# An adaLN block with dilated local attention and a SiLU FFN: rows of 448 held as four overlapping tiles of 128

## The chip, the cores and the metric

The kernel runs on one core of a Trainium2 chip. A core has TensorE (PE in the profile; its weight loads are the row PEld), VectorE (DVE), ScalarE (ACT), GpSimd (POOL) and SyncE (SP, which here only issues DMAs). They run side by side, each in its own fixed order, and wait for each other through semaphores. The metric is the device time of one execution in microseconds (us), lower is better. Times of one instruction are given in us or ns as the profile has them.

## The reference

One transformer layer, sequence 2048, width 448, 16 heads of 28, FFN width 1792, all inputs bf16:

```python
mod = silu(c) @ w_mod                      # 448 -> 6 * 448: sa, ca, ga, sb, cb, gb
h = layernorm(x) * (1 + ca) + sa
x = x + ga * attention(h)                  # qkv = h @ wqkv; out = o @ wo
h = layernorm(x) * (1 + cb) + sb
x = x + gb * (silu(h @ w1) @ w2)
```

Attention is local and dilated: position s sees s, s-2, ..., s-14 (8 keys, those below 0 masked), with logits scaled by 28^-0.5 and a softmax over the 8.

## The kernel before

**Tiling.** The sequence is split by parity into two streams of 1024, so that the dilated window becomes 8 neighbours. It is worked in four chunks (`NC`) of 2 x 256 positions, and attention in nine blocks (`BLOCKS`) of 128 keys and 112 queries (128 for block 0), for each parity. A width of 448 is contracted on TensorE as three tiles of 128 rows and a rest of 64. `tile 3` of a transposed activation holds rows 384 to 447 in 64 partitions. Matmuls on 64 partitions come in pairs, one on the lower half of the array and one on the upper half, so the rest has to be present in both halves: each modulation (L491 to L497, L513 to L519) writes it twice, once to partitions 0 to 63 and once to 64 to 127. The weights' rests (`wqkv3`, `w13`) are loaded to the two halves by two DMAs each. `xn` is 512 wide with 64 zero columns.

**Stages of a chunk.** Statistics of x (`stat`, L428, on DVE), reciprocal square root on POOL (`rstd`, L442 to L449), the normalized rows `xn` (`norm`, L456 on ACT or L458 on DVE), a transpose (chunk 0: on TensorE, L486; others: DMA transposes issued by SP, L510), the modulation (`mod`). Then the q and k projections (`project`, L596, two groups of 16 matmuls, each over two large PSUM buffers), whose results ACT or DVE evict (L600), and v (L620, evicted at L609). For each block and parity: logits (L648), exp on ACT (L656), mask on DVE (L680), attention times v (L706), normalization on DVE (L712), DMA transpose of o (L716). Output projection (L740), and addition to x with the row sums (L743). The FFN of a chunk: sums and squares for the second norm (L438 on ACT), transposes by DMA, modulation (L519 on DVE, L517 on ACT), first matrix with SiLU on ACT (L766, L768, L772), second matrix (L790), addition (L795), store.

**PSUM.** Three large buffers (`big`, two banks each) serve the transposes of chunk 0, q/k and v projections, logits, output projection and the FFN's first matrix. Two small ones (`one`) serve attention times v, the modulation's matmuls and the FFN's second matrix.

**The start.** 11 matmuls on zeros (`WARM`, L369) and then 3 (`JUNK`) behind each of chunk 0's four transposes keep TensorE active until data is there. The modulation vectors need `w_mod` (two DMAs for the first part); `pad` (L525 to L530) spreads the q/k weights of 28 columns a head to 32.

**Order.** The work is written as steps (`P.op`) with a cost and dependencies. A planner can order them, but for the kernel that runs, the order is given by the string `ORDER`: the numbers of the steps, with `v` (DVE) or `a` (ACT) where a step may go to either. Each engine gets its instructions in that order. `SEQ` sets the order in which attention blocks (e) and FFN chunks (s) are created, with one switch of ACT's table (exp or SiLU) at each change. In the string before, attention of blocks 0 to 3 comes ahead of FFN chunk 0, blocks 4 and 5 among its second matrix, 6 to 8 among that of FFN chunk 1.

Of the kernel before, what the change touches and what calls it, by code (L numbers as in the profile page):

```python
# [10 lines left out]
ALU = mybir.AluOpType  # L11
# [4 lines left out]
D = 448  # L16
H = 16
DH = 28
F = 1792
# [16 lines left out]
WARM, JUNK = 11, 3  # L36
HOW1 = ("bbbb", "bbbb", "bbbb", "bbbb")
HOW2 = ("ssss", "ssss", "ssss", "ssss")
SEQ = "e0 e1 e2 e3 s0 e4 e5 s1 e6 e7 e8 s2 s3"
# [3 lines left out]
    "0 4 5 91 79 3 2 1 80 81 92 93 94v 65 66 67 68 69 8 6 7 95a 82 83 9 96 97 98 99v 10 11 101 102 12 15 13 21 19 17 14 18 22 85 89v 86 87v 100a 16 20 90a "  # L43
    "88a 103 104 106v 105a 114 74 73 70 78 71 116a 29 30 158a 141 115 142 143 144a 145a 31 27 25 23 107 32 146 147 33 37 24 28 117 26 176 148 72 175 149v "
    "181 177 39 180 178v 151 40 34 209 215 118a 150a 152 108 109 119 153 110a 112a 179v 84 156v 155v 154v 157v 192v 210 35 59 49 111 182 75 76 50 113 120 "
    "121a 63 47 45 183v 214 184v 38 186 185 55 41 43 42 36 46 48 211 245 122 246 123a 124 125v 247 212a 248 165 166 169v 130 167a 213a 132 77 216 168 170 "
    "264 265 266 252 253 254 249 267 250 191v 255 171 268 172a 217a 188a 269 159 219 131 61 251 62 161a 190v 189v 162 44 160 163v 164 271 256 272 273 126 "
    "279 280 281 64 257 274 218v 127v 282 205 259 286 275 206a 287 288 276 277 187 270 173 283 57 220 278 58 289 284 285 174a 133 260 261 262 263 56 258 "
    "298 290 299 300 291 301 223v 128 305 306 207 307 317 319 208a 137 225v 293 302 303 129 308 222a 318 226a 199 201a 320 294 224a 309 51 304 53 136 296 "
    "295 310 311 323 221 324 325 52 202 312 54 292 60 297 200 203a 139 321v 322v 204 329 193 194 195a 197a 198 326 134 328v 327v 138 330 313 314 315 316 "  # L50
    "196 331 334a 332v 239 241 333v 335v 354 427 242a 429 140 240v 342 343 355 344 346 345 356 336 337 338 428 430 431v 135 339 347 340 348 349 350 341 "
    "351 389 357 358 352 359 365 353 390 391 396 397 392 360 366 398 408 409 410 361 367 399 393 415 394 416 368 417 400 395 369 401 227 228 418 229a 231a "
    "232 230 411 419 420 432a 403 422 439 404 406 405 433 434 435 436 402 381 412 243 413 414 438v 407 233 234 373 437v 440 442v 445v 443v 235a 244a 423 "
    "382 237a 424 425 362 363 364 238 236 370 426 371 444a 464 465 466 458 460 461 372 459 556 462 446 447 448 450 558 449 463 452 453 454 455 451 499 383 "
    "384 385 374 375 376 456 386 457 500 501 377 506 467 468 507 502 503 504 518 508 557 559 469 470 519 525 509 378 505 379 380 471 510 511 483 484 485 "
    "486 560a 520 526 521 522 527 561a 512 528 487 523 537 513 421 387 388 514 538 539 515 516 529 491 544 492 562 564 563 565 530 493 494 488 568 524 545 "
    "546 441 489 517 531 540 495 532 566v 567v 475 541 569 476 533 542 547 548 477 478 574a 573v 571v 572v 575 576 534 535 628 630 629 631 490 536 549 577 "
    "496 543 551 632v 633v 640 578 593 552 579 479 700 594 553 554 634 635 636 637 639v 638v 641 595 580 620 581 604 582 583 645v 643v 480 472 646v 644v "
    "584 555 587 588 585 589 591 586 592 590 621 605 622 606 607 647 648 623 473 497 498 474 649 650 653 654 624 596 597 657 658 608 651 655 625 609 610 "
    "570 656 652 642 626 627 481 611 665 676 598 599 600 601 602 482 603 659 660 661 666 663 677 692 693 694 695 678 679 696 680 681 697 698 668 669 612 "  # L60
    "613 614 615 670 699 682 616 671 672 673 617 684 685 686 687 618 683 688 667 674 619 675 664 662 550 689 690 701 702 703 691 "
# [12 lines left out]
def half(j):  # L74
    return slice(K3 * j, K3 * j + K3)


def rows_of(k, j=0):

    return half(j) if k == 3 else slice(0, 128)  # L80
# [118 lines left out]
def layer(ctx, tc, io, safe):  # L199
# [3 lines left out]

# [33 lines left out]
    wv = ct([128, 3, D], "wv")  # L237
    wqkv3 = ct([128, 2, D], "wqkv3")
# [43 lines left out]
    for i in range(2):  # L282
        V.memset(ob[0][i][:, D:512], 0.0)
        V.memset(ob[1][i][:, 0:K3], 0.0)
        V.memset(xn[i][:, :, D:512], 0.0)
# [21 lines left out]

    begin = P.op(("sp", 1630.0), none)

    def load(kb, out, in_, after=()):  # L310
        a = P.op(("sp", max(400.0, kb / 0.31)), lambda o: nc.sync.dma_start(out=out, in_=in_), [begin] + list(after))
        return P.op(("none", 500.0), none, [a])
# [13 lines left out]
    ld_ma = load_mod(0, 2 * D + K3)  # L326
    late = [P.op(("sp", 800.0), none, ld_ma[:1])]
    rest = A_wqkv[384:D, :].rearrange("k (a n) -> k a n", a=3)
    ld_qk = [[load(224, wqk[:, kk, :], A_wqkv[128 * kk:128 * kk + 128, 0:2 * D], late)] for kk in range(3)]
    ld_qk.append([load(56, wqkv3[half(j), 0, :], rest[:, j, :], late) for j in range(2)])  # L330
    ld_v = [load(336, wv[:], rows3(A_wqkv[:, 2 * D:3 * D]), late)] + [load(56, wqkv3[half(j), 1, :], rest[:, 2, :], late) for j in range(2)]
    ld_x += [[load(448, x_all[:, 4 * k:4 * k + 4, :].rearrange("p (i t) d -> p i (t d)", t=2), x_view[k], late)] * 2 for k in range(1, NC)]
    ld_mo, ld_mb, ld_m2 = load_mod(2 * D + K3, 3 * D, late), load_mod(3 * D, 5 * D + K3, late), load_mod(5 * D + K3, 6 * D, late)
    ld_m2 = ld_mb + ld_m2
    ld_o = [load(336, wo[:, 0, 0:3, :], rows3(A_wo), late), load(56, wo[half(0), 0, 3, :], A_wo[384:D, :], late)]
    ld_1 = [load(448, w1[:, kk, :], B_w1[128 * kk:128 * kk + 128, :], late) for kk in range(3)]
    ld_1 += [load(112, w13[half(h), :], B_w1[384:D, h * F // 2:(h + 1) * F // 2], late) for h in range(2)]
# [31 lines left out]
    w_last = P.op(("pe", 213.0 * WARM), lambda o: warm_up(WARM), [w_first], mac=213.0 * WARM)  # L369

# [7 lines left out]
    cc = P.op(("pe", 60.0), c_cols, [sc_op, w_last], take=("one",))  # L378
# [3 lines left out]
    def mod_cols(vecs, dst0, loads):  # L382
# [3 lines left out]
        def mm(o):  # L386
            ps[0] = one.tile([128, 2, KT], F32, name="ps_m", tag="one")
            for i, v in enumerate(vecs):
                for j in range(KT):
                    c0 = v * D + 128 * j  # L390
                    for k in range(KT):
                        T.matmul(ps[0][:, i, j:j + 1], lhsT=wmod[:, k, c0:c0 + 128], rhs=scT[:, k:k + 1], start=(k == 0), stop=(k == KT - 1))
# [23 lines left out]
    class Norm:  # L416


        def __init__(self, us, src, after=(), n=2, how="bbbb", scratch=None):
# [31 lines left out]
            def norm(o, j, b):  # L451
                if j == 0:
                    self.box["x"] = xn[o["slot"]["xn"]]
                out_, in_ = self.box["x"][:, j, 0:D], x_all[:, us[j], :]
# [5 lines left out]
            for j in range(0, 4, n):  # L460
# [8 lines left out]
                for i in at:  # L469
                    self.nr.append(P.op(either(640.0, 310.0), lambda o, j=i, b=b: norm(o, j, b), [r] + self.nr[:1], take=() if i else ("xn",)))  # L470

        def on_pe(self, order, out_of, view, waits, junk_n=0, two=False):
# [6 lines left out]
            def tr(o, j):  # L479
# [7 lines left out]
                if junk_n:  # L487
                    warm_up(junk_n)
# [81 lines left out]
    def norm1(k):  # L570
# [5 lines left out]
        def out_of(rows, kt):  # L576
            return h[rows, :, kt, 128:128 + CP]
# [346 lines left out]
```

## Time and profile before

| | us |
|---|---|
| median of 14 runs (185.12 to 187.61) | 186.94 |
| the profiled execution | 187.28 |
| its span, first to last instruction | 185.4 |
| mean granted TensorE clock | 0.983 |

The span is what the trace covers; 1.9 us of the profiled execution lie around it. Groups of the page that the change bears on, each with the line, engine, operation, result and operand, shapes and count, then busy us in total and mean ns of one, then the idle time before them and what ended it:

```profile
L456 ACT ACTIVATE xn<-x_all,nm,rs 128x448 bf16<-128x448 bf16 x11 | 8.3, 760 | 8.5 <-POOL nm L449 6.8 <-POOL nm L447 1.8
L458 DVE TENSOR_SCALAR xn<-x_all,mv,rs 128x448 bf16<-128x448 bf16 x21 | 7.6, 388 | 18.0 <-POOL rs L445 17.9
L519 DVE TENSOR_SCALAR h<-h,modc 128x512 bf16<-128x512 bf16 x14 | 5.2, 408 | 8.5 <-DMA h<-xn 8.5
L519 DVE TENSOR_SCALAR h<-h,modc 64x512 bf16<-64x512 bf16 x10 | 4.1, 405 | 0.3
L517 ACT ACTIVATE h<-h,modc 128x512 bf16<-128x512 bf16 x4 | 3.3, 832 | 2.8 <-DMA h<-xn 2.8
L367 PE MATMUL ps_w<-both 128*128 128x512 bf16 x22 | 7.5, 486 | 1.3 <-DVE both L272 1.2
```

The norms read 448 elements a row, the modulations write 512 columns, on 128 partitions or, for the rest, on 64. `ps_w` are the matmuls on zeros.

### The profile page before, as it was taken

How to read it: one execution, taken by the hardware profiler on the slowest of the kernel's cores; microseconds unless marked ns; L12 is line 12 of the kernel's file. 1: busy time of each engine (PE TensorE's matmuls, PEld its weight loads, DVE VectorE, ACT ScalarE, POOL GpSimd, SP SyncE). 2: the span in 40 equal slices, each digit the busy share in tenths (PEclk: the TensorE clock that was granted, in tenths of full speed). 3: DMA queues.
4: the chain of work that ended last, by engine and by line, in shares of the span. 5: the costliest groups of instructions: out<-in, count | busy, mean ns of one | idle time of the engine just before them, and what ended most of it. 6: DMA issues, size and time to landing. Idle time of an engine off the chain costs nothing.

```text
span 185.4 us, 3540 instructions
## 1 busy us (share of the span) xinstructions
PE 169.7 (92%) x1401; PEld 76.8 (41%) x1402; DVE 97.2 (52%) x223; ACT 115.5 (62%) x151; POOL 28.5 (15%) x86
## 2 busy tenths in 40 slices
PE   7769896999999999999999999989989999999950
PEld 2333333345643333454443345455334444445520
DVE  7579888968997802097433015788752222012120
ACT  3176979788899597896385689666496611650000
POOL 1736536000043002000200000402022000000000
PEclk9999999699999999999999999999999999999997
DMA  5995698979465200002440001223421501000120
GB/s 177 327 339 183 149 279 173 240 224 172 104 147 160 57 0 4 0 0 53 106 108 4 0 0 50 55 55 79 106 57 24 108 2 50 0 25 4 50 74 16
DMA packets 33119, 17.42 MB, mean 94 GB/s; under 512 B 24328, under 2 KB 32584, under 8 KB 33096
## 3 DMA queue, kind: packets, MB, share of 16 engines
q1 hardware_dynamic: 33088, 17.13, 36.6%
q8 instruction: 13, 0.21, 0.5%
q14 instruction: 10, 0.08, 0.2%
q10 hardware_dynamic: 8, 0.00, 0.0%
HBM read 9.12 MB, written 1.84 MB: 59 GB/s over the span
## 4 chain that ended last, share of the span: by engine, by line
PE 53%; ACT 18%; DVE 9%; POOL 6%; DMA 5%; issue 4%; SPq 1%; ACTq 0%; DVEq 0%; POOLq 0%
PE ps_h L766 18%; PE ps_y L790 12%; PE ps_qk L596 8%; ACT p L656 6%; PE ps_v L620 5%; PE ps_wo L740 4%; PE ps_h L768 4%; DMA h<-xn 3%; ACT screp L438 3%; POOL rs L445 2%; ACT xn L456 2%; PE ps_o L706 2%; DMA w<-in_B_w_dram 2%; ACT both L772 2%; DVE x_all L743 2%
## 5 line engine op out<-in xcount | busy, mean ns | idle before, releaser
L790 PE MATMUL ps_y<-w,both 128*128 128x448 bf16 x224 | 46.1, 353 | 0.2 <-DVE o L712 0.2
L772 ACT ACTIVATE both<-ps_h 128x1024 bf16<-128x1024 f32 x28 | 27.9, 1023 | 20.2 <-PE ps_h L768 12.2
L766 PE MATMUL ps_h<-h,w 128*128 128x512 bf16 x168 | 40.2, 380 | 0.2 <-DVE h L519 0.2
L656 ACT ACTIVATE p<-ps_l 128x896 bf16<-128x896 f32 (+1 forms) x36 | 30.8, 936 | 2.2 <-PE ps_l L648 2.1
L795 DVE TENSOR_TENSOR ot<-ps_y,x_all 128x448 bf16<-128x448 f32 x16 | 9.9, 622 | 38.2 <-PE ps_y L790 38.2
L790 PEld LDWEIGHTS <-both 128*128 128x128 bf16 x224 | 20.8, 98 | 19.9 <-issue 0.9
L766 PEld LDWEIGHTS <-w 128*128 128x128 bf16 x168 | 15.3, 98 | 22.1 <-issue 6.1
L680 DVE TENSOR_TENSOR p<-p,maskb 128x1792 bf16<-128x1792 bf16 (+1 forms) x18 | 19.7, 1101 | 8.1 <-ACT p L656 8.0
L596 PE MATMUL ps_qk<-h,wp 128*128 128x512 bf16 (+1 forms) x96 | 21.2, 390 | 1.2 <-ACT h L495 1.2
L600 ACT CAST qk<-ps_qk 128x1024 bf16<-128x1024 f32 x14 | 13.9, 1011 | 5.3 <-PE ps_qk L596 5.2
L458 DVE TENSOR_SCALAR xn<-x_all,mv,rs 128x448 bf16<-128x448 bf16 x21 | 7.6, 388 | 18.0 <-POOL rs L445 17.9
L596 PEld LDWEIGHTS <-wp 128*128 128x128 bf16 (+1 forms) x128 | 9.5, 98 | 17.2 <-issue 8.9
L438 ACT ACTIVATE screp<-x_all,mv 128x448 bf16<-128x448 bf16 x16 | 10.7, 671 | 6.1 <-POOL mv L435 5.8
L519 DVE TENSOR_SCALAR h<-h,modc 128x512 bf16<-128x512 bf16 (+1 forms) x24 | 9.1, 407 | 8.8 <-DMA h<-xn 8.5
L456 ACT ACTIVATE xn<-x_all,nm,rs 128x448 bf16<-128x448 bf16 x11 | 8.3, 760 | 8.5 <-POOL nm L449 6.8
L740 PE MATMUL ps_wo<-wo,oT 128*128 128x448 bf16 (+1 forms) x64 | 13.0, 354 | 0.5 <-ACT both L772 0.5
L712 DVE TENSOR_TENSOR o<-ps_o,rc 112x448 bf16<-112x448 f32 (+1 forms) x18 | 11.2, 624 | 0.6
L445 POOL TENSOR_TENSOR rs<-rs,negh 128x2 f32<-128x2 f32 x16 | 11.3, 709 | 1.3
L706 PEld LDWEIGHTS <-p 128*128 128x128 bf16 x288 | 9.1, 96 | 4.9 <-DVE p L680 1.8
L706 PE MATMUL ps_o<-v,p 128*128 128x29 bf16 x288 | 10.1, 176 | 0.9 <-DVE p L680 0.7
L435 POOL TENSOR_SCALAR mv<-sums 128x2 f32<-128x2 f32 x8 | 1.7, 218 | 58.9 <-DVE x_all L743 58.9
L743 DVE SCALAR_TENSOR_TENSOR x_all<-ps_wo,x_all 128x448 bf16<-128x448 f32 x16 | 9.3, 619 | 1.9 <-PE ps_wo L740 1.9
(86 smaller groups left out, 159.2 us busy)
## 6 DMA issues: line engine op xcount, KB each, us to landing
out_dram<-ot SPq DMA_DIRECT2D x16, 112.0 KB, 1.8
both<-in_w_mod_dram SPq DMA_DIRECT2D x2, 720.0 KB, 4.3
x_all<-in_A_x_dram SPq DMA_DIRECT2D x3, 448.0 KB, 5.7
w<-in_B_w_dram SPq DMA_DIRECT2D x3, 448.0 KB, 4.5
w<-in_B_w_dram SPq DMA_DIRECT2D x1, 896.0 KB
wqk<-in_A_wqkv_dram SPq DMA_DIRECT2D x3, 224.0 KB, 4.7
w<-in_B_w_dram SPq DMA_DIRECT2D x1, 672.0 KB, 5.9
both<-in_w_mod_dram SPq DMA_DIRECT2D x2, 288.0 KB, 4.3
```

The source lines that it names most:

```text
L438: S.activation(out=scratch, in_=x_all[:, us[j], :], func=ACTF.Square, bias=mv[:, j, 0:1], accum_out=mv[:, j, 1:2])
L445: G.tensor_tensor(out=rs[:, j:j + n], in0=rs[:, j:j + n], in1=negh[:, 0:n], op=ALU.pow)
L596: T.matmul(ps[:, j, :], lhsT=w.rearrange("p h d -> p (h d)"), rhs=h[rows_of(kk, j), :, kk, 128:128 + CP], start=start, stop=stop)
L600: return [(either(act_ns(1024), dve_ns(1024)), lambda o, ps: copy_on(o)(out=qk[:, :, g, :, s0:s0 + CP], in_=ps[:].rearrange("p j (t s) -> ...
L656: S.activation(out=out_, in_=ps[:, :, 0:4 * nq].rearrange("p j (g q) -> p j g q", q=nq), func=ACTF.Exp, scale=SCALE)
L680: V.tensor_tensor(out=p, in0=p, in1=maskb[:, 1 if b == 0 else 0, 0:nq].unsqueeze(1).to_broadcast([128, H, nq]), op=ALU.mult)
L706: T.matmul(ps[:, h, 0:DH + 1], lhsT=p[:, at:at + 128], rhs=v[:, h, 0:DH + 1], start=True, stop=True)
L740: T.matmul(ps[:, par, 0:D], lhsT=oT[rows, kk, par, s0:s0 + 128], rhs=wo[rows, par, kk, :], start=(q == qs[0]), stop=(q == qs[-1]))
L743: V.scalar_tensor_tensor(out=x_all[:, u + par, :], in0=box["ps"][:, par, 0:D], scalar=1.0, in1=x_all[:, u + par, :], op0=ALU.mult, op1=ALU ...
L766: T.matmul(ps[:, j, :], lhsT=w1[:, kk, c0:c0 + 128], rhs=h[:, :, kk, :], start=start, stop=stop)
L772: return [(("act", act_ns(1024)), lambda o, ps: S.activation(out=hid[:, k % 2, :, i, :], in_=ps[:], func=ACTF.Silu), after + f2_read.get(k ...
L790: T.matmul(box["ps"][:, 0:D], lhsT=hid[:, k % 2, f % 2, f // 2, 128 * j:128 * j + 128], rhs=w2[:, f // 2 + 7 * (f % 2), :], start=(f == 0) ...
```

## The change

The rows of a 448-wide activation are held as four tiles of 128 that overlap: rows 0 to 127, 128 to 255, 192 to 319 and 320 to 447 (`ROW`). The norm writes 512 columns, reading columns 0 to 255 and 192 to 447 of x (`overlap`). A contraction then has two ways (`tile_of`): way 0 takes tiles 0, 1, 3 in full and rows 256 to 319 from the upper half of tile 2; way 1 takes tiles 0, 2, 3 in full and rows 128 to 191 from the lower half of tile 1. The pairs of 64-row matmuls use one way each, so both halves of the array have their rest without a second copy. The modulation has one instruction per tile, also in chunk 0; the number of matmuls and their sizes stay. The output projection keeps its old scheme.

The weights are loaded to match (`dram` makes access patterns of HBM by row, column and count): wqk by 3 DMAs, not 5, of which one holds both rests; v's weights by 2, not 3; the FFN's rests by 1, not 2. The first part of `w_mod` has 896 columns, not 960.

The warm-up has 6 matmuls and then 8 steps of 2, which the order places one by one. The planner counts 8 DMAs in flight as a resource; with a given order this changes nothing that runs. The zeroing of `xn`'s last 64 columns goes.

`ORDER` is new throughout. At the start: x's second half is loaded ahead of `w_mod`; all four statistics of chunk 0 come ahead of DVE's norms; POOL's masks and fillings come ahead of its first reciprocal square root; the modulation's matmuls come ahead of the four transposes, 8 of the small warm-up matmuls behind them. Then the projection of chunk 0 (groups 0 and 2), v of block 0, logits, v of blocks 1, 2 and 3 with logits between them, both projections of chunk 1 and the first of chunk 2, logits of block 2, and so on. FFN chunk 0 follows attention of blocks 0 to 4; 5 and 6 lie among its second matrix, 7 at the start of FFN chunk 1, 8 behind it. V is evicted by DVE for six blocks (before: one), 15 norms (before: 11) and 9 modulations are on ACT.

```diff
-WARM, JUNK = 11, 3
+WARM, JUNK = 6, 8
-SEQ = "e0 e1 e2 e3 s0 e4 e5 s1 e6 e7 e8 s2 s3"
+SEQ = "e0 e1 e2 e3 e4 s0 e5 e6 s1 e7 e8 s2 s3"
 ORDER = (
...
 )
-def rows_of(k, j=0):
-    return half(j) if k == 3 else slice(0, 128)
+ROW = (0, 128, 192, 320)
+def tile_of(k, way):
+    return (slice(0, 128), (0, 1 + way, 3)[k]) if k < 3 else (half(1 - way), 2 - way)
+def overlap(ap):
+    return bass.AP(ap.tensor, ap.offset, [list(ap.ap[0]), [192, 2], [1, 256]])
+def dram(ap, row, col, dims):
+    w = ap.ap[0][0]
+    return bass.AP(ap.tensor, ap.offset + row * w + col, [[r * w + c, n] for r, c, n in dims])
...
-    wv = ct([128, 3, D], "wv")
-    wqkv3 = ct([128, 2, D], "wqkv3")
+    wv = ct([128, KT, D], "wv")
+    wqk3 = ct([128, D], "wqk3")
-        V.memset(xn[i][:, :, D:512], 0.0)
...
-    ld_ma = load_mod(0, 2 * D + K3)
-    late = [P.op(("sp", 800.0), none, ld_ma[:1])]
-    rest = A_wqkv[384:D, :].rearrange("k (a n) -> k a n", a=3)
-    ld_qk = [[load(224, wqk[:, kk, :], A_wqkv[128 * kk:128 * kk + 128, 0:2 * D], late)] for kk in range(3)]
-    ld_qk.append([load(56, wqkv3[half(j), 0, :], rest[:, j, :], late) for j in range(2)])
-    ld_v = [load(336, wv[:], rows3(A_wqkv[:, 2 * D:3 * D]), late)] + [load(56, wqkv3[half(j), 1, :], rest[:, 2, :], late) for j in range(2)]
+    ld_ma = load_mod(0, 2 * D, [x["deps"][0] for x in ld_x[0]])
+    late = [P.op(("sp", 800.0), none, [x["deps"][0] for x in ld_ma])]
+    a = load(448, wqk[:, 0:3:2, :], dram(A_wqkv, 0, 0, ((1, 0, 128), (320, 0, 2), (0, 1, 2 * D))), late)
+    b = load(224, wqk[:, 1, :].rearrange("p (a n) -> p a n", a=2), dram(A_wqkv, 128, 0, ((1, 0, 128), (64, D, 2), (0, 1, D))), late)
+    ld_qk = [[a], [b], [a], [load(112, wqk3[:], dram(A_wqkv, 128, D, ((128, -D, 2), (1, 0, K3), (0, 1, D))), late)]]
+    ld_v = [load(224, wv[:, 2 * a:2 * a + 2, :], dram(A_wqkv, 192 * a, 2 * D, ((1, 0, 128), (128, 0, 2), (0, 1, D))), late) for a in range(2)]
-    ld_mo, ld_mb, ld_m2 = load_mod(2 * D + K3, 3 * D, late), load_mod(3 * D, 5 * D + K3, late), load_mod(5 * D + K3, 6 * D, late)
-    ld_m2 = ld_mb + ld_m2
+    ld_mo, ld_mb, ld_m2 = load_mod(2 * D, 3 * D, late), load_mod(3 * D, 5 * D, late), load_mod(5 * D, 6 * D, late)
-    ld_1 = [load(448, w1[:, kk, :], B_w1[128 * kk:128 * kk + 128, :], late) for kk in range(3)]
-    ld_1 += [load(112, w13[half(h), :], B_w1[384:D, h * F // 2:(h + 1) * F // 2], late) for h in range(2)]
+    ld_1 = [load(448, w1[:, k, :], B_w1[r:r + 128, :], late) for k, r in ((0, 0), (2, 320))]
+    ld_1.append(load(448, w1[:, 1, :].rearrange("p (a n) -> p a n", a=2), dram(B_w1, 128, 0, ((1, 0, 128), (64, F // 2, 2), (0, 1, F // 2))), late))
+    ld_1.append(load(224, w13[:], dram(B_w1, 128, F // 2, ((128, -(F // 2), 2), (1, 0, K3), (0, 1, F // 2))), late))
...
+    junks = [P.op(("pe", 428.0), lambda o: warm_up(2), [w_last], mac=426.0) for _ in range(JUNK)]
+    P.op(("none", 0.0), none, junks, give=((w_first, "big"),))
...
-    cc = P.op(("pe", 60.0), c_cols, [sc_op, w_last], take=("one",))
+    cc = P.op(("pe", 60.0), c_cols, [sc_op], take=("one",))
...
-                    c0 = v * D + 128 * j
+                    c0 = v * D + ROW[j]
...
-                out_, in_ = self.box["x"][:, j, 0:D], x_all[:, us[j], :]
+                out_, in_ = self.box["x"][:, j, :].rearrange("p (a n) -> p a n", a=2), overlap(x_all[:, us[j], :])
...
-                if junk_n:
-                    warm_up(junk_n)
             def mod(o, i, ks):
-                for k, to, from_ in [(k, slice(0, 128), slice(0, 128)) for k in ks if k < 3] + [(3, half(h), half(0)) for h in range(2) if 3 in ks]:
-                    out_, in_ = out_of(to, k), view(box[i][from_, k - ks[0], :])
-                    scale, shift = modc[from_, 1, k:k + 1], modc[from_, 0, k:k + 1]
+                for k in ks:
+                    out_, in_ = out_of(k), view(box[i][:, k - ks[0], :])
+                    scale, shift = modc[:, 1, k:k + 1], modc[:, 0, k:k + 1]
...
-                trs.append(P.op(("pe", 240.0 + 213.0 * junk_n), lambda o, j=j: tr(o, j), [self.nr[j]] + (trs[-1:] or self.after), take=() if j else ("big",) * len(parts),
-                                give=((self.nr[0], "xn"),) if j == 3 else (), mac=213.0 * (1 + junk_n)))
+                trs.append(P.op(("pe", 240.0), lambda o, j=j: tr(o, j), [self.nr[j]] + (trs[-1:] or self.after), take=() if j else ("big",) * len(parts),
+                                give=((self.nr[0], "xn"),) if j == 3 else (), mac=213.0))
...
-                for to, from_ in ([(half(1), half(0)), (half(0), half(0))] if k == 3 else [(slice(0, 128),) * 2]):
-                    out_, in_ = out_of(to, k), out_of(from_, k)
-                    scale, shift = modc[from_, vec + 1, k:k + 1], modc[from_, vec, k:k + 1]
-                    if o["eng"] == "act":
-                        S.activation(out=out_, in_=in_, func=ACTF.Identity, scale=scale, bias=shift)
-                    else:
-                        V.tensor_scalar(out=out_, in0=in_, scalar1=scale, scalar2=shift, op0=ALU.mult, op1=ALU.add)
-            trs = [P.op(("sp", 1250.0), lambda o, j=j: tr(o, j), self.nr[j:j + 2] + self.after) for j in (0, 2)]
+                scale, shift = modc[:, vec + 1, k:k + 1], modc[:, vec, k:k + 1]
+                if o["eng"] == "act":
+                    S.activation(out=out_of(k), in_=out_of(k), func=ACTF.Identity, scale=scale, bias=shift)
+                else:
+                    V.tensor_scalar(out=out_of(k), in0=out_of(k), scalar1=scale, scalar2=shift, op0=ALU.mult, op1=ALU.add)
+            trs = [sp(1250.0, lambda o, j=j: tr(o, j), self.nr[j:j + 2] + self.after)[0] for j in (0, 2)]
-            self.done = [P.op(either(670.0 * (1 + (k == 3)), 340.0 * (1 + (k == 3))), lambda o, k=k: mod(o, k), trs + list(waits)) for k in range(KT)]
+            self.done = [P.op(either(670.0, 340.0), lambda o, k=k: mod(o, k), trs + list(waits)) for k in range(KT)]
...
-                w = wp[:, kk, H * j + 4 * g:H * j + 4 * g + 4, :] if kk < 3 else wp3[half(j), 4 * g:4 * g + 4, :]
-                T.matmul(ps[:, j, :], lhsT=w.rearrange("p h d -> p (h d)"), rhs=h[rows_of(kk, j), :, kk, 128:128 + CP], start=start, stop=stop)
+                rows, t = tile_of(kk, j)
+                w = wp[:, kk, H * j + 4 * g:H * j + 4 * g + 4, :] if kk < 3 else wp3[rows, 4 * g:4 * g + 4, :]
+                T.matmul(ps[:, j, :], lhsT=w.rearrange("p h d -> p (h d)"), rhs=h[rows, :, t, 128:128 + CP], start=start, stop=stop)
...
-                        w = wv[:, kk, :] if kk < 3 else wqkv3[half(par), 1, :]
-                        T.matmul(ps[:, par, 0:D], lhsT=h[rows_of(kk, par), par, kk, b0:b0 + 128], rhs=w, start=(kk == ks[0]), stop=(kk == ks[-1]))
+                        rows, t = tile_of(kk, par)
+                        T.matmul(ps[:, par, 0:D], lhsT=h[rows, par, t, b0:b0 + 128], rhs=wv[rows, t, :], start=(kk == ks[0]), stop=(kk == ks[-1]))
...
-                if kk < 3:
-                    c0 = 128 * (i + 7 * j)
-                    T.matmul(ps[:, j, :], lhsT=w1[:, kk, c0:c0 + 128], rhs=h[:, :, kk, :], start=start, stop=stop)
-                else:
-                    T.matmul(ps[:, j, :], lhsT=w13[half(j), 128 * i:128 * i + 128], rhs=h[half(j), :, 3, :], start=start, stop=stop)
+                rows, t = tile_of(kk, j)
+                c0 = 128 * (i + 7 * j)
+                w = w1[:, kk, c0:c0 + 128] if kk < 3 else w13[rows, 128 * i:128 * i + 128]
+                T.matmul(ps[:, j, :], lhsT=w, rhs=h[rows, :, t, :], start=start, stop=stop)
```

## The prediction

> **What bounds the kernel now.** I read the busy table first, then the slices, the chain of waits, a table of windows by stage, and the timeline of the first 60 us.
>
> ```profile
> PE 169.7 (92%) x1401; PEld 76.8 (41%) x1402; DVE 97.2 (52%) x223; ACT 115.5 (62%) x151; POOL 28.5 (15%) x86
> PEclk9999999699999999999999999999999999999997
> PE 53%; ACT 18%; DVE 9%; POOL 6%; DMA 5%; issue 4%; SPq 1%; ACTq 0%; DVEq 0%; POOLq 0%
> 0.00:13.80 13.80, 9.77 (x72) 4.46 (x74) 9.15 (x30) 5.79 (x9) 5.61 (x26) 1.00 0.88 280
> 13.80:29.10 15.30, 14.09 (x85) 5.49 (x85) 13.66 (x39) 12.28 (x15) 8.12 (x25) 1.00 0.74 202
> 29.10:32.50 3.40, 2.17 (x51) 1.41 (x51) 2.81 (x3) 3.40 (x6) 1.91 (x3) 1.00 0.88 173
> 32.50:35.90 3.40, 3.40 (x25) 1.21 (x24) 3.26 (x8) 2.99 (x5) 0.00 (x0) 0.50 1.23 288
> 35.90:63.20 27.30, 26.74 (x322) 13.30 (x321) 23.04 (x52) 21.73 (x31) 3.93 (x9) 1.00 0.71 151
> ```
>
> The last five rows are windows (width, busy us of PE, PEld, DVE, ACT, POOL, granted clock). TensorE is the bound: the other engines are busy 52% and 62%, and the matmuls of the result are not touched by the change. So the span is four pieces. Before the projections start: 13.8 us. From there to 63.2 us, TensorE is busy 14.09 + 2.17 + 3.40 + 26.74 = 46.4 of 49.4 us: **3.0 us idle**. In it one window of 3.4 us ran at clock 0.50, which costs 3.4 / 2 = **1.7 us**. From 63.2 to 178.6 three more windows are busy 54.12, 20.80 and 38.60 of 115.4 us: **1.9 us idle**. The tail (last matmul, addition, store, end) is 6.8 us, and its steps stay. 13.8 + 49.4 + 115.4 + 6.8 = 185.4. Only 13.8 + 3.0 + 1.7 + 1.9 us can be had at all.
>
> **The start, 13.8 us.** The timeline shows what comes last there:
>
> ```profile
> 9.89 0.39 DVE L527 COPY wp<-wqk 128x896 bf16<-128x896 bf16 x1
> 10.33 0.51 DVE L527 COPY wp<-wqk 128x896 bf16<-128x896 bf16 x1
> 10.40 0.76 ACT L456 ACTIVATE xn<-x_all,nm,rs 128x448 bf16<-128x448 bf16 x1 [2.47 <-POOL nm L449]
> 11.21 0.40 PE L486 MATMUL ps_t<-ident,xn 128*128 128x128 bf16 x4
> 11.52 0.93 ACT L527 COPY wp<-wqk 128x896 bf16<-128x896 bf16 x1
> 11.65 1.56 DVE L497 TENSOR_SCALAR h<-ps_t,modc 128x512 bf16<-128x512 bf16 x3 [0.81 <-PE ps_t L486]
> 12.36 1.44 ACT L495 ACTIVATE h<-ps_t,modc 128x512 bf16<-128x512 bf16 x2
> 13.84 6.41 PE L596 MATMUL ps_qk<-h,wp 128*128 128x512 bf16 x31 [0.29 <-ACT h L495]
> ```
>
> The chain is statistics, rsqrt on POOL, last norm (10.40), transposes (11.21), modulation, projections. Before, VectorE puts a norm, which waits for POOL, between its second and third statistics. The new order runs all four statistics first, and x's second half is loaded before the modulation matrix. By rows: the two `xn` memsets (0.17 us each) go, so statistics start at about 3.6 (x is first used at 3.86); four at 0.73 end at 6.5. POOL takes 1.56 us a pair (5.53 to 7.09): pairs end at 6.7 and 8.3. The last norm runs on ACT 8.3 to 9.1 and the last transposes 9.1 to 9.5, 2.1 us earlier. VectorE's modulation has two instructions, not three (2 x 0.52), done at 10.6; ACT's follows one short pad (0.55), 9.6 to 11.0. VectorE then pads two pieces (0.45 each): 11.5. TensorE could start at 11.4, against 13.6 before (31 matmuls from 13.84, one ahead of them): **-2.2 us**. The 8 warm-up pieces ahead of it, 16 matmuls at 0.22, fill 9.5 to 11.3 and cost nothing at full clock.
>
> [...] The new load of the 64-row rests of wqk, `wqk3`, reads DRAM with a count of 2 outermost (so does `w13`). No load in this trace has that. The nearest rows are the old rests (wqkv, 56 KB, two halves), which land 3.2 to 5.3 us after issue, like the full-height loads (4.6 to 4.9): by them nothing is lost. [...]
>
> **Fewer, wider elementwise steps.** 8 chunks lose one modulation each (the 64x512 halves cost as much as a full one: 405 against 408 ns). 32 norms read 512, not 448: +20 ns on VectorE (388 to 408), about +55 on ACT (760 to the 813-832 of its 512-wide modulation). The two-segment read of the norm is the shape of the modulation at 408 ns, so I expect no slower mode. The order shifts 5 of the V evictions (0.91 ACT, 1.08 DVE) to VectorE and 4 norms and 3 modulations to ACT. Totals: ACT about -0.5, VectorE about +1 us. Both have 60 us and more of idle time: nothing by themselves. On the path it is one modulation per FFN chunk, and there TensorE has other work (12 us of it ahead of FFN chunks 2 and 3).
>
> **The new order, 13.8 to 63 us.** Attention blocks 0 to 4, not 0 to 3, now come before FFN chunk 0, and chunk 2's first projection is moved ahead of block 2. Logits need two of three large PSUM buffers, released by exp (ACT, 0.86 apart), an eviction or the x1 additions (VectorE). I walked the new sequences of PE, ACT and VectorE with the spacings of the trace (eviction 0.92, exp 0.86, ACT norm 0.72, mask 1.02, normalization of o 0.78, VectorE eviction 1.14; projection of 16 matmuls 3.3, V 1.6, logits 0.4, AV 0.4, output projection 1.43), counted from the first projection. TensorE waits 1.25 us between 8 and 13 us (first evictions, the exp table load of 1.28), 0.65 at 18 to 23, 0.65 at 31 to 37, and 1.75 at 41 to 47: there two pairs of logits follow each other and ACT also has norms and squares in its queue. Sum **4.3 against 3.0, +1.3 us**; bounds -1 (each wait may overlap a semaphore latency I counted) and +3.5 (half as long again, and a later transpose). SP: `T1` for chunk 2 stands behind a transpose of o that waits for block 0; it lands at about 24 from the start, when ACT wants it (0.2 late). The copies of wo are issued near 27 and land by 31 (before: 5.0 us in a fuller queue, then 32); the output projection wants them at 31.8.
>
> **The clock.** Before, the window with 2.17 us of TensorE work in 3.4 (29.1 to 32.5) is followed by one at 0.50; windows with 2.25 (5.2 to 8.6) and 2.29 are not. [...] I take half, **-0.85**; ends -1.7 and +1.7 (a drop in the start too: its 5.2 to 8.6 now has one-column matmuls and transposes, and fewer 512-wide ones).
>
> **From 63 us on.** Fewer blocks are left to compete with FFN chunk 1; the walk gives 0.4 idle at the switch of FFN chunk 0 to block 6 and little later: 1.4 against 1.9, **-0.5** (ends -1, +1).
>
> **Sum:** -1.2 + 1.3 - 0.85 - 0.5 = -1.25 us on the profiled 187.28 (span 185.4 and 1.9 around it): 186.0. That execution is 0.3 above the median of the runs, 186.94; on the median it is 185.7.
>
> **Rivals.**
> [...]
> *No change, 186.9:* the start gains 1.2, the waits eat it (1.3), and half clock stays once. For it: five blocks in a row on three buffers.
> *Slower, 189.1:* the three large PSUM buffers between 8 and 47 us after the start. If each wait is half as long again (6.45, +3.45 on before), with half clock after the sparse stretch as before and the start at -1.2: +2.2. It decides once that idle time passes 3.0 + 1.2 + 0.9 = 5.1 us. For it: ACT is 80% busy from 13.8 to 63.2 us already (40.4 of 49.4). Against: before has the same waits (logits waiting at 29.46, 30.18 and 30.93 for three releases) and pays 3.0.
>
> **Numbers.** Chances: forecast 0.40, more gain 0.22, no change 0.17, slower 0.21. A difference of 0.5% (0.93 us) is about what this measurement can tell from none. The forecast's own spread (184.4 to 186.8) lies four fifths below 186.0, so faster 0.55, within 0.5% 0.22, slower 0.23. The range 182.9 to 188.8 leaves out part of the slower case and the ends of the best.
>
> **What would show it.** [...] PEclk shows one slice at 6 or none. Modulations number 8 fewer plus one in the start. It is wrong if the norms with overlapping reads take much more than 410 ns, if TensorE waits for a transpose, or if a half-clock window lies in the first 14 us.

## The result and the profile after

The kernel after takes 184.18 us (median of 10 runs, 182.78 to 185.63), the kernel before 186.46 in the same comparison (47 runs, 185.12 to 188.3). The ratio is 0.988, with a 95% interval from 0.9847 to 0.9914: 1.2% faster. The profiled execution took 184.85 us, its span is 183.1. Here and below a median is of all runs listed, while a ratio leaves out every run more than 1.5% above the fastest of its kernel: one each in the kernel after, e5, e6 and e7, three of six in e1, three of twelve in e8, its profiled execution among them.

From the page of the kernel after: busy time by engine, the granted clock in 40 slices, the chain of waits.

```profile
PE 168.5 (92%) x1400; PEld 77.4 (42%) x1401; DVE 97.0 (53%) x213; ACT 115.7 (63%) x151; POOL 27.7 (15%) x86
PEclk9969999999999999999999999999999999999997
PE 68%; DMA 10%; DVE 10%; ACT 4%; issue 2%; SPq 2%; POOL 1%; DVEq 0%; ACTq 0%
```

Shares of busy time hardly differ from before. The chain does: ACT falls from 18% to 4% and DMA rises from 5% to 10%. The clock's slice at 6 has moved from the eighth of the 40 to the third, into the start. The timeline of the start (start, us, engine, line and operation, and in brackets the idle time ahead and its releaser) shows where the DMA share lies:

```profile
8.78 0.23 PE L417 MATMUL ps_m<-scT,both 128*128 128x1 bf16 x3 [1.73 <-DMA both<-in_w_mod_dram]
...
11.28 0.56 ACT L550 COPY wp<-wqk 128x448 bf16<-128x448 bf16 x1 [2.15 <-DMA wqk<-in_A_wqkv_dram]
...
12.99 0.39 DVE L548 COPY wp<-wqk 128x896 bf16<-128x896 bf16 x1 [2.43 <-DMA wqk<-in_A_wqkv_dram]
...
13.30 0.99 DVE L520 TENSOR_SCALAR h<-ps_t,modc 128x512 bf16<-128x512 bf16 x2
14.21 0.69 DVE L548 COPY wp<-wqk 128x896 bf16<-128x896 bf16 x2
...
14.65 0.82 PE L617 MATMUL ps_qk<-h,wp 128*128 128x512 bf16 x3 [0.27 <-DVE wp L548]
```

VectorE waits 2.43 us for wqk with a pad at the head of its queue. Two modulations and two more pads stand behind that pad, and the first projection behind them all. It starts at 14.65; before, the projections ran on from 13.84. **The start became 0.8 us longer, not shorter.** What was won lies behind it. Windows of the kernel after (width, busy us of PE, PEld, DVE, ACT, POOL, clock, DMA share, GB/s):

```profile
6.34:9.75 3.41, 1.29 (x21) 0.62 (x19) 0.90 (x4) 1.62 (x2) 1.80 (x8) 1.00 1.02 284
9.75:13.17 3.42, 3.20 (x40) 2.59 (x38) 0.41 (x3) 1.89 (x3) 0.00 (x0) 0.50 1.07 355
14.65:63.20 48.55, 45.69 (x520) 21.40 (x522) 43.29 (x90) 40.54 (x53) 12.80 (x33) 1.00 0.76 158
63.20:118.00 54.80, 54.35 (x448) 24.29 (x449) 25.39 (x54) 42.31 (x56) 5.35 (x14) 1.00 0.22 58
118.00:140.00 22.00, 21.03 (x178) 9.83 (x177) 12.15 (x26) 15.11 (x20) 2.83 (x9) 1.00 0.21 51
140.00:176.40 36.40, 36.40 (x188) 16.48 (x185) 7.78 (x19) 12.35 (x16) 1.31 (x4) 1.00 0.15 44
```

The half-clock window is now the one from 9.75 to 13.17; from the first projection to the last matmul the clock is full. (From 1.24 to 5.6 us the views show 1.00 too, but the warm-up matmuls follow each other at 0.43 us there, as in the half-clock window of e3 below, and at 0.22 in e1 from 9.45 on, at full clock. From these spacings I estimate that the span starts at half clock.) Idle time of TensorE to 63.2 us is 48.55 - 45.69 = 2.9 us.

A measure that serves for all kernels of this study is **the stretch**: from the moment from which the projections run on to the last small matmul of the tail (`ps_f`). Each row is one window of one profiled execution:

| kernel | projections run on from | stretch | TensorE busy in it | idle in it |
|---|---|---|---|---|
| before | 13.84 | 164.61 | 159.78 | 4.83 |
| after | 14.65 | 161.79 | 157.51 | 4.28 |
| e5: before, rests in one load | 13.87 | 164.47 | 158.79 | 5.68 |
| e9: new tiles, old order | 13.88 | 164.59 | 159.81 | 4.78 |
| e8: after, one more step a chunk | 14.97 | 164.91 | 158.26 | 6.65 |
| e10: after, load of rests last | 13.90 | 160.96 | 157.27 | 3.69 |
| e1: after, load of rests split | 11.75 | 161.61 | 157.47 | 4.14 |
| e12: split, and more warm-up | 12.53 | 161.03 | 157.34 | 3.69 |

So the change won 2.8 us on the stretch, lost 0.8 in the start and won 0.35 behind `ps_f`: 2.36 of span. Only 0.55 of the 2.8 is idle time; 2.3 is busy time. A row is one execution: those of e8 and e9 are 1.3 and 1.5 us slower than the medians of their runs, those of e1 and e10 2.3 and 1.2 us faster.

### The profile page after: what moved, and what is told of

Same layout as the page of the kernel before. It is cut to its first block, busy times and chain, and to the rows that moved or that the text cites. A ratio compares the mean times of both kernels' runs of the same rounds, so it can differ in the third digit from the quotient of the medians.

```text
span 183.1 us, 3526 instructions
## 1 busy us (share of the span) xinstructions
PE 168.5 (92%) x1400; PEld 77.4 (42%) x1401; DVE 97.0 (53%) x213; ACT 115.7 (63%) x151; POOL 27.7 (15%) x86
## 4 chain that ended last, share of the span: by engine, by line
PE 68%; DMA 10%; DVE 10%; ACT 4%; issue 2%; SPq 2%; POOL 1%; DVEq 0%; ACTq 0%
PE ps_h L788 25%; PE ps_y L810 21%; PE ps_qk L617 9%; PE ps_wo L761 6%; DMA wqk<-in_A_wqkv_dram 5%; PE ps_v L641 4%; DMA h<-xn 3%; DVE p L701 2%; ACT p L677 2%; DMA oT<-o 2%; PE ps_l L669 2%; PE ps_o L727 2%; SPq L334 2%; DVE qk L621 1%; DVE h L540 1%
## 5 line engine op out<-in xcount | busy, mean ns | idle before, releaser
L788 PE MATMUL ps_h<-h,w 128*128 128x512 bf16 (+1 forms) x224 | 47.4, 380 | 0.9 <-DVE h L540 0.9
L810 PE MATMUL ps_y<-w,both 128*128 128x448 bf16 x224 | 45.2, 353 | 0.0
L788 PEld LDWEIGHTS <-w 128*128 128x128 bf16 (+1 forms) x224 | 17.4, 97 | 27.1 <-issue 10.4
L617 PE MATMUL ps_qk<-h,wp 128*128 128x512 bf16 (+1 forms) x96 | 20.3, 380 | 0.7 <-DVE v L630 0.4
L621 ACT CAST qk<-ps_qk 128x1024 bf16<-128x1024 f32 x13 | 12.9, 1009 | 4.8 <-PE ps_qk L617 4.7
L460 POOL TENSOR_SCALAR mv<-sums 128x2 f32<-128x2 f32 x8 | 2.9, 365 | 77.5 <-DVE x_all L764 77.5
L540 DVE TENSOR_SCALAR h<-h,modc 128x512 bf16<-128x512 bf16 x17 | 6.4, 406 | 14.4 <-DMA h<-xn 14.4
L481 ACT ACTIVATE xn<-x_all,nm,rs 128x512 bf16<-128x512 bf16 x15 | 12.0, 809 | 2.9 <-POOL nm L472 1.4
L641 PE MATMUL ps_v<-wv,h 128*128 128x448 bf16 (+1 forms) x56 | 11.0, 354 | 0.6 <-ACT v L630 0.6
L483 DVE TENSOR_SCALAR xn<-x_all,mv,rs 128x512 bf16<-128x512 bf16 x17 | 6.6, 404 | 6.7 <-POOL rs L470 6.7
```

What stands on the lines that cost most here:

```text
L481: S.activation(out=out_, in_=in_, func=ACTF.Identity, scale=rs[:, j:j + 1], bias=nm[:, j:j + 1])
L617: T.matmul(ps[:, j, :], lhsT=w.rearrange("p h d -> p (h d)"), rhs=h[rows, :, t, 128:128 + CP], start=start, stop=stop)
L621: return [(either(act_ns(1024), dve_ns(1024)), lambda o, ps: copy_on(o)(out=qk[:, :, g, :, s0:s0 + CP], in_=ps[:].rearrange("p j (t s) -> ...
L641: T.matmul(ps[:, par, 0:D], lhsT=h[rows, par, t, b0:b0 + 128], rhs=wv[rows, t, :], start=(kk == ks[0]), stop=(kk == ks[-1]))
L788: T.matmul(ps[:, j, :], lhsT=w, rhs=h[rows, :, t, :], start=start, stop=stop)
L810: T.matmul(box["ps"][:, 0:D], lhsT=hid[:, k % 2, f % 2, f // 2, 128 * j:128 * j + 128], rhs=w2[:, f // 2 + 7 * (f % 2), :], start=(f == 0) ...
```

## The experiments

### The start: is it the load of the rests?

My theory was that `wqk3`, one DMA whose source has a count of 2 outermost, holds up by its form what is queued behind it. The rival was that the loads are late for a reason that has nothing to do with the form of this one, a slow spell between 3.5 and 5 us (146 GB/s there, against 383 in the kernel before).

**e1: the same bytes in two DMAs of 64 rows.**

```diff
-load(112, wqk3[:], dram(A_wqkv, 128, D, ((128, -D, 2), (1, 0, K3), (0, 1, D))), late)
+two(112, wqk3, (A_wqkv[128:192, D:2 * D], A_wqkv[256:320, 0:D]), late)   # one DMA for each half
```

> The changed kernel with the rests of wqk loaded by two DMAs of 64 rows in place of one with a count of 2 outermost. [...] Rival, memory stall: the slow spell of the loads between 3.5 and 5 us does not depend on this load's shape; the first projection stays at 14 or later and the time within 0.4 us of the changed kernel (184.2).

Measured: 183.96 us (6 runs, 181.67 to 185.97), ratio 0.9823 [0.9767, 0.9879], of three runs. The timeline of its profile, which is of the fastest of the six:

```profile
10.09 0.40 DVE L555 COPY wp<-wqk 128x896 bf16<-128x896 bf16 x1 [1.13 <-DMA wqk<-in_A_wqkv_dram]
...
11.31 0.69 DVE L555 COPY wp<-wqk 128x896 bf16<-128x896 bf16 x2
...
11.75 5.03 PE L624 MATMUL ps_qk<-h,wp 128*128 128x512 bf16 x24 [0.41 <-DVE wp L555]
```

The pad that waited until 12.99 runs at 10.09, and the first projection starts 2.9 us earlier by nothing but the form of one load. The DMA issues agree (size, median us from issue to landing), first two of the kernel after, then two of e1:

```profile
wqk<-in_A_wqkv_dram SPq DMA_DIRECT2D x1, 448.0 KB, 9.0
wqk<-in_A_wqkv_dram SPq DMA_DIRECT2D x1, 224.0 KB, 8.2
...
wqk<-in_A_wqkv_dram SPq DMA_DIRECT2D x1, 448.0 KB, 5.3
wqk<-in_A_wqkv_dram SPq DMA_DIRECT2D x1, 224.0 KB, 4.7
```

So e1 shows the form of the load as the cause; by what way the form does it, no view here shows. The time followed by less than the start: by the ratios e1 is 1.1 us below the kernel after, with overlapping intervals, and the runs lie 4.3 us apart. The warm-up experiments bear on that.

**e3: the FFN's rests `w13` split in the same way, on top of e1.** The edit is the same at `ld_1`.

> Both rest loads (wqk's and the FFN's w13) as two DMAs of 64 rows each, the order as in the changed kernel. Theory: only wqk's rests lie on the path, so this is as the run with them alone: first projection at 11.7 to 12.2 us, ratio to before 0.979 to 0.985 (182.6 to 183.6). [...]

Measured: 183.85 us (6 runs, 182.72 to 184.32), ratio 0.9861 [0.9812, 0.991]. No gain beyond e1 shows: `w13` was free, as I had expected. But in this profile the first projection started at 13.57, not 11.75.

**e10: the load not split, but issued behind the other wqk pieces** (steps 17 and 18 moved behind 13 and 14 in `ORDER`).

> The changed kernel with the single load of wqk's rests issued behind the other two pieces of wqk, not ahead of them. [...] Rival: what matters is the number of bytes ahead; the first projection stays at 14 or later.

Measured: 184.85 us (10 runs), ratio 0.9917 [0.988, 0.9954]. The pieces behind it are freed (VectorE's first pad at 10.21), but ACT's pad of the rest itself waits until 11.93, its modulations follow, and the projections run on from 13.90. So the slow load costs as the last one too, by its own landing. The start is 0.75 us earlier than in the kernel after, and the time is not lower. The profiled execution (183.61) is the fastest of the ten, so it may show less than the others had; why the median doesn't follow stays open.

**e5: the kernel before with its two q/k rest loads joined into one with a count of 2.**

```diff
-[load(56, wqkv3[half(j), 0, :], rest[:, j, :], late) for j in range(2)]
+pair = bass.AP(A_wqkv.tensor, A_wqkv.offset + 384 * 3 * D, [[D, 2], [3 * D, K3], [1, D]])
...
+load(112, wqkv3[:, 0, :], pair, late)
```

> The kernel before with its two q/k rest loads (56 KB each) joined into one with a count of 2 outermost, all else as it was. [...] Rival, memory stall: one DMA fewer and no other difference, the time stays within 0.5 us of 186.5.

Measured: 186.64 us (12 runs), ratio 1.0005 [0.9976, 1.0035]: no change, where I had expected the form of the load to cost time here as well. The timeline of its profile:

```profile
11.53 0.93 ACT L529 COPY wp<-wqk 128x896 bf16<-128x896 bf16 x1
11.68 0.40 DVE L529 COPY wp<-wqk 128x896 bf16<-128x896 bf16 x1 [1.72 <-DMA wqk<-in_A_wqkv_dram]
...
12.37 1.44 ACT L497 ACTIVATE h<-ps_t,modc 128x512 bf16<-128x512 bf16 x2
...
13.87 1.24 PE L598 MATMUL ps_qk<-h,wp 128*128 128x512 bf16 x5 [0.29 <-ACT h L497]
```

The load is late here too: VectorE's pad runs at 11.68, not at 9.89. But TensorE waits for ACT's two modulations, from 12.37 to 13.81, which are as late without it (12.36 before). The delay of 1.8 us fits under another chain. A load of the same form is free in one kernel and costs 2.9 us of start in the other.

### The warm-up: where does the half clock fall?

**e6: the last 8 small warm-up matmuls (4 steps) ahead of the modulation's matmuls**, not behind the transposes.

```diff
-... 101a 86 102 96v ... 33 34 73 75 77 148 74 81 ...
+... 101a 73 75 77 74 86 102 96v ... 33 34 148 81 ...
```

> The changed kernel with the 8 warm-up matmuls that stand behind the four transposes moved ahead of the modulation's matmuls, where TensorE waits for w_mod (6.6 to 8.8 us). Loads theory: the window of half clock (9.75 to 13.17 us) goes, but the start waits for the weights' landing and not for TensorE, so the first projection stays within 0.4 us of 14.65 and the time within 0.5 us of 184.2. Rival, clock theory: half clock in the start is what makes it late; the first projection comes 1 us or more earlier and the time falls by 0.8 to 1.7 us.

Measured: 185.94 us (12 runs), ratio 0.997 [0.9939, 1.0], some 1.7 us above the kernel after. The first projection hardly moves (14.52). Two windows of its profile:

```profile
10.70:14.11 3.41, 0.72 (x13) 0.55 (x10) 1.32 (x6) 1.91 (x3) 0.00 (x0) 1.00 1.08 352
14.11:17.53 3.42, 3.01 (x8) 0.87 (x10) 3.28 (x11) 0.00 (x0) 0.39 (x2) 0.50 1.08 318
```

Here TensorE is nearly empty before the projections (0.72 us of 3.41), and the half clock falls on the projections (14.11 to 17.53); in the kernel after, with the pieces behind the transposes, it falls on transposes and pieces (9.75 to 13.17) while VectorE waits for the load. By its clock of 0.50 I estimate that the window could cost up to 3.42 / 2 = 1.7 us, but this trace does not show that it did: its stretch, from 14.52, is 161.90 us with TensorE busy 158.61, so 1.1 us more busy time than in the kernel after, 1.0 less idle time, and 0.1 longer. The loss of the runs has another part that no trace shows. This execution (185.05) is the third fastest of the twelve, with a mean clock of 0.985; ten of the twelve have 0.969 to 0.978, so more half clock than this trace.

**e7: e6 with both loads of rests split.**

> Both rests (wqk and the FFN's w13) loaded by two DMAs each, and the 8 warm-up matmuls moved ahead of the modulation's matmuls. [...] Rival, memory stall: within 0.5 us of 184.2.

Measured: 183.51 us (6 runs), ratio 0.9812 [0.9775, 0.9848]; first projection at 12.63, and half clock on the projections (0.50 from 12.70 to 16.10). Here the window shows in the stretch: 162.12 us, against 160.84 in e11 below, whose loads are the same and whose projections have full clock. With early loads the late pieces are not clearly worth anything: in e3, which has them, the half clock fell on the pieces themselves, and those held up the projection, ready by about 12.5, until 13.57. Two windows of e3:

```profile
7.00:10.40 3.40, 2.33 (x50) 1.89 (x50) 0.65 (x3) 2.04 (x4) 1.31 (x5) 1.00 1.05 331
10.40:13.80 3.40, 3.26 (x9) 1.21 (x8) 3.13 (x8) 1.42 (x2) 0.00 (x0) 0.50 1.08 348
```

So the question for a better version was whether to move pieces or to add some.

**e11: e3 with 4 of the 8 pieces moved ahead of the modulation's matmuls.**

> The changed kernel with both loads of rests split in two, and of the 8 warm-up matmuls behind the transposes 4 moved ahead of the modulation's matmuls. With all 8 behind, a half-clock window over them held the first projection at 13.57 instead of 11.75 us in one profile. If the warm-up pieces behind the transposes are what is dear at half clock: 4 cost at most 1.8 us at half clock and 0.9 at full, so the first projection starts at 11.7 to 12.4 in every case; median 182.5 to 183.5 (ratio 0.976 to 0.984). If instead the work between 8 and 12 us has to be dense for full clock on the projections: half clock falls on the projections, and the time is that of the changed kernel with the split loads and all 8 behind, or above, 183.9 to 185.

Measured: 182.72 us (6 runs, 181.92 to 183.66), ratio 0.979 [0.9738, 0.9843]. Its profile has full clock (1.00) in every window from 5 us to 176, behind the last matmul, though the projection starts only at 12.82, later than I had written, behind VectorE's pads.

**e12: e3 with 4 more matmuls ahead, and all 8 behind.**

```diff
-junks = [P.op(... warm_up(2) ...) for _ in range(JUNK)]
+junks = [P.op(... warm_up(n) ...) for n in (2, 2, 2, 2, 2, 4, 4, 2)]
```

> The changed kernel with both loads of rests split in two, and 4 more warm-up matmuls ahead of the modulation's matmuls; all 8 stay behind the transposes. If a sparse stretch between 7 and 10 us calls for the half clock: TensorE is now busy 0.9 us more there, no half-clock window in the first 17 us, first projection at 11.7 to 12.2, median 182.3 to 183.3 (ratio 0.975 to 0.983). If the half clock does not depend on these 0.9 us: half clock over the warm-up matmuls behind the transposes or over the first projections as in the other kernels, first projection at 11.7 to 13.6, median 183.7 to 185.

Measured: **181.95 us** (6 runs, 180.33 to 182.3), ratio 0.9714 [0.9659, 0.9768], below both kernels: 0.9714 against the kernel before, where the kernel after has 0.988 and the two intervals do not meet. Two windows of its profile:

```profile
6.00:9.40 3.40, 2.65 (x46) 1.72 (x45) 1.48 (x6) 1.89 (x3) 2.06 (x9) 1.00 1.08 293
9.40:12.80 3.40, 2.57 (x21) 1.26 (x18) 1.93 (x6) 1.64 (x3) 0.00 (x0) 1.00 1.07 379
```

All its six runs have a mean clock of 0.991 to 0.996; those of e3 have 0.978 to 0.986. So 0.9 us of TensorE work on zeros did away with a half-clock window in the start, as far as the mean clocks tell, and the time fell by 1.9 us against e3 (2.7 by the ratios). How the one makes the other is in part open: the two profiled executions, the slowest of e12's six and the fastest of e3's, are only 0.4 us apart, with the first projection 1.0 us earlier (12.53) and the stretch 0.6 us longer, and half of one window's length is only 1.7.

### Behind the start: the order, or the steps saved?

The prediction called the fewer elementwise steps "nothing by themselves" and put all of its sum on the order. Its rival was that VectorE and ACT stand behind the waits, so that each step saved shows.

**e8: the kernel after with one step more in each chunk.** It rewrites 64 rows of tile 3 in place behind tile 3's modulation, and the matmuls wait for it, as they waited for the second copy before. The values stay.

```diff
+if k == 3: dup = out_of(k)[half(1)]
+    V.tensor_scalar(out=dup, in0=dup, scalar1=1.0, scalar2=0.0, ...)   # or S.activation, where the modulation is on ACT
```

> The changed kernel with one further elementwise step of 64 rows in each of the eight modulations of tile 3 (an exact copy in place, on the engine that did the modulation, and the matmuls wait for it): the saved instructions are paid again, 0.4 us each on VectorE or 0.8 on ACT. Order theory: they lie beside TensorE's other work, the time stays within 0.5 us of the changed kernel (184.2). Elementwise theory: the gain comes from the saved steps, the time rises by 1.2 to 2.3 us.

Measured: 187.26 us (12 runs), ratio 1.0017 [0.9973, 1.0062], 2.5 us more than the kernel after: the whole gain is gone. The steps themselves are small: 5 on VectorE of 0.29 us and 3 on ACT of 0.63, 3.3 us on two engines. Of the stretch's 3.1 us more, 2.4 are idle time of TensorE. At the start it is plain, in the timeline of e8's profile:

```profile
13.17 0.99 DVE L520 TENSOR_SCALAR h<-ps_t,modc 128x512 bf16<-128x512 bf16 x2
14.20 0.29 DVE L522 TENSOR_SCALAR h<-h 64x512 bf16<-64x512 bf16 x1
14.52 0.70 DVE L556 COPY wp<-wqk 128x896 bf16<-128x896 bf16 x2
14.97 1.25 PE L625 MATMUL ps_qk<-h,wp 128*128 128x512 bf16 x5 [1.35 <-DVE wp L556]
```

Later the same happens to a mask or an eviction behind the step; the longest new wait, 0.83 us at 47.59, is for a copy of wo by DMA, whose issue had moved from 41.1 to 42.4. The profiled execution (188.55) is 1.3 us above the median, so its rows show the places; the size is from the runs. And e8 gives the price of a step in this order, in which each step had its place without it; e9 gives the tiles without the order.

**e9: the new tiles with the order before, step for step**, and split loads.

> The four overlapping tiles and the new loads (rests by two DMAs each), but the order of before, step for step: attention of blocks 0 to 3 ahead of FFN chunk 0, the same engine for each step that had a choice, the warm-up behind the transposes. Order theory: the time is that of before within 0.6 us (185.9 to 187.1), as ACT's modulation in the start is as long as before. Structure theory: the tiles alone give it, 184.8 or less.

Measured: 185.33 us (12 runs), ratio 0.9938 [0.9901, 0.9974], between the two theories. Its start is that of the kernel before (13.88) and so is its stretch, but in an execution 1.5 us above the median, with a half-clock window (164.59), so where the tiles gain is not shown. By the ratios the new tiles alone gain 0.6%, the new order with a step put back gains nothing, and both together gain 1.2% with a start that is 0.8 us longer (1.4% with the loads split as in e9, which is e3). The order pays only with the shorter queues.

## Why the prediction was right, and where its steps were not

The forecast was faster, 185.7, by -1.25 us; measured on the profiled executions it is 187.28 - 184.85 = -2.4. That the direction and the rough size came out is in good part luck. By the two traces the change is +0.8 in the start, -0.55 of TensorE's idle time behind it, -2.27 of its busy time and -0.35 behind `ps_f`. The forecast was 2.0 us too good for the start and 1.4 too bad for the walk, which cancel for the larger part, and some 1.6 us of the gain stand in no term of it.

**The start (-1.2) went the other way, +0.8.** No run shows the -1.2; in its place the runs showed 14.65 with the load in one DMA and 11.75 (e1) with it split. The form of the load delays the loads behind it (9.0 and 8.2 us to landing, 5.3 and 4.7 in e1). And I had put VectorE's pads behind its modulations; the pad waited until 12.99 and stood ahead of them in VectorE's queue, so 0.99 of modulation and 0.69 of pads came after the landing. The start as the rows of before gave it, -2.2 or 11.4, is near what e1 shows: 11.75. `w_mod` also lands 6.9 us after issue, not 4.3; with the split it is 5.8 in e1, so part of that is not the rests' doing. Which part is not settled.

**The walk of the new order (+1.3) gave -0.1.** Waits of TensorE in the kernel after, from its timeline:

```profile
23.72 1.61 PE L641 MATMUL ps_v<-wv,h 64*128 64x448 bf16 x8 [0.63 <-ACT v L630]
26.51 0.37 PE L669 MATMUL ps_l<-qk 28*128 28x112 bf16 x14 [0.23 <-DVE v L630]
31.89 3.39 PE L617 MATMUL ps_qk<-h,wp 128*128 128x512 bf16 x16 [0.35 <-DVE v L630]
45.35 1.59 PE L761 MATMUL ps_wo<-wo,oT 128*128 128x448 bf16 x8 [0.24 <-ACT p L677]
56.47 0.38 PE L669 MATMUL ps_l<-qk 28*128 28x112 bf16 x16 [0.96 <-DVE qk L621]
59.78 0.57 PE L727 MATMUL ps_o<-v,p 128*128 128x29 bf16 x16 [0.26 <-DVE p L701]
```

Counted from 14.65 they lie at 9 and 12, 17, 31, and 42 and 45 us: near the four places of the walk. The sizes are 0.86, 0.35, 0.24 and 1.22 against 1.25, 0.65, 0.65 and 1.75, some 60%. The likely reason, which no run tests, is the latencies counted twice: the allowance for them had been made as a bound (-1) and not in the value. The slower rival needed more than 5.1 us of idle time (5.55, had its limit counted the forecast's own -0.5 behind 63 us), and 2.9 were there.

**The clock (-0.85).** The window at 32.5 is gone, as the forecast half had it, but its price of 1.7 us was too high. Of the 57 runs of the kernel before that the ratios of the experiments use, 37 have a mean clock of 0.986 or more, with a median of 186.02, and 20 a lower one, with 187.14: 1.1 us. (The mean takes in the lower clock behind the last matmul, 0.80 from 178.6 us on in the profiled execution, so it is a sign of a window and not a count.) The profiled execution was one of the 20. e5, whose profile has no such window, shows why it is not 1.7: TensorE is busy 1.0 us less in its stretch and idle 0.85 more, so the stretch is only 0.14 shorter. The faster matmuls then wait for the same evictions. And a window lies in the start now, an end that I had named and not taken. In the kernel after, the sparsest stretch of 3.41 us between 14.65 and 63 us, counted on from the half-clock window, is 54.13 to 57.54 with 2.45 us of work; it was followed by full clock. Going by busy time was the wrong measure, as the last section shows.

**The elementwise steps ("nothing by themselves") is the step that fell**: e8, 2.5 us. And e9 puts the tiles at 0.6% in the old order, not at nothing. I had argued from 60 us of idle time on each engine, a share over the whole span, while in the stage that counts VectorE is busy for 87% and ACT for 82%. The kernel before:

```profile
13.84:63.20 49.36, 46.40 (x480) 21.41 (x480) 42.74 (x99) 40.41 (x53) 13.96 (x37) 0.97 0.77 178
```

The prediction had ACT's share among its rivals and did not draw this from it. The norm itself was as expected:

```profile
L540 DVE TENSOR_SCALAR h<-h,modc 128x512 bf16<-128x512 bf16 x17 | 6.4, 406 | 14.4 <-DMA h<-xn 14.4
L481 ACT ACTIVATE xn<-x_all,nm,rs 128x512 bf16<-128x512 bf16 x15 | 12.0, 809 | 2.9 <-POOL nm L472 1.4
...
L483 DVE TENSOR_SCALAR xn<-x_all,mv,rs 128x512 bf16<-128x512 bf16 x17 | 6.6, 404 | 6.7 <-POOL rs L470 6.7
```

404 ns on VectorE and 809 on ACT, against 408 and about 815.

**From 63 us on (-0.5):** idle 0.68 + 1.20 before, 0.45 + 0.97 after: -0.46, as forecast. The windows before:

```profile
63.20:118.00 54.80, 54.12 (x466) 23.71 (x465) 21.25 (x43) 41.24 (x51) 4.84 (x11) 1.00 0.12 30
118.00:140.00 22.00, 20.80 (x189) 10.02 (x188) 15.88 (x35) 15.86 (x23) 2.74 (x9) 1.00 0.31 73
```

**What the sum did not have:** "only 13.8 + 3.0 + 1.7 + 1.9 us can be had at all" took TensorE's busy time as fixed. In the stretch it is 157.51 after and 158.79 in e5, both at full clock: 1.3 us less for the same matmuls. e9, with the old order, has 159.81 with one half-clock window, which speaks for the order and not the tiles; but e8, in the new order, has 158.26, so the order alone does not fix it. What makes the difference stays open. Ends of matmuls are modelled in the profile, so part of it may be the accounting.

**Slips of the working.** The warm-up behind the transposes is 8 matmuls and not 16: 16 of 0.22 would be 3.5 us, and 9.5 to 11.3 holds 8. And of the range 184.4 to 186.8 two thirds lie below 186.0, if all of it is equally likely, not four fifths. Neither moved the forecast.

## What to carry to other kernels

A load that is the same bytes in fewer DMAs can be slower by microseconds: here two pieces queued behind it landed 9.0 and 8.2 us after issue, and 5.3 and 4.7 with it split (e1). Look at how long what is queued behind it takes to land, and ask what stands behind its consumer in that consumer's queue, since that decides whether the delay costs nothing (e5) or 2.9 us of start (e1). Judge an engine's slack in the stage that bounds the kernel and not over the span: 3.3 us of small steps, spread over two engines that are idle for 60 us and more, cost 2.5. And do not price a half-clock window at half its length, 1.7 us here, without looking at what runs in it and behind it: matmuls that then wait less for evictions pay less (0.14 us of stretch in before against e5, 0.1 in e6 against after, 1.3 in e7 against e11), and work on zeros pays nothing unless it holds up the real work.

## What the runs showed of the hardware that was not expected

**A window need not be idle to be followed by half clock, and busy time did not decide it here.** Three stretches of the kernel before, each as long as its half-clock window of 3.41 us, with the one behind each:

```profile
5.21:8.62 3.41, 2.26 (x18) 0.98 (x17) 1.97 (x6) 0.81 (x2) 2.71 (x10) 1.00 1.05 324
8.62:12.04 3.42, 2.96 (x47) 1.80 (x46) 1.65 (x6) 1.64 (x3) 2.13 (x9) 1.00 0.99 320
12.04:15.45 3.41, 2.20 (x11) 0.69 (x10) 3.24 (x9) 1.75 (x3) 0.48 (x2) 1.00 1.07 350
15.45:18.86 3.41, 3.41 (x19) 1.27 (x18) 3.27 (x11) 3.39 (x5) 2.92 (x10) 1.00 0.25 93
...
29.11:32.52 3.41, 2.19 (x51) 1.43 (x51) 2.82 (x3) 3.41 (x6) 1.91 (x3) 1.00 0.89 177
32.52:35.93 3.41, 3.41 (x26) 1.20 (x25) 3.27 (x8) 3.00 (x5) 0.00 (x0) 0.50 1.27 283
```

2.26 and 2.20 us of TensorE were followed by full clock, 2.19 by half; in e3, 2.33 us (7.00 to 10.40) were followed by half clock. The matmuls differ too: 18, nine of them with 512 columns, and 11, all with 512, against 51, of which 30 are logits on 28 rows and 16 attention times v with 29 columns. Whether that is what decides is not shown.

**The same start comes out differently from run to run.** With the split loads and the same warm-up order, the modulation's matmuls waited for `w_mod` until 7.52 in e1 and until 8.40 in e3. e1 has full clock from 5.00 to 15.40; e3 has half clock from 10.40 to 13.80, and its first projection at 13.57 and not 11.75. In e12, with 4 more matmuls, the clock is full from 5.00 to 176.00. So one profile is a poor measure of a start.
